# Moving the exponential, the query and key splits and the conversion copies within a step of a fused attention and expert kernel

## The chip, the cores and the metric

One core of one Trainium2 chip. The metric is device time in microseconds (us) of one launch; lower is better. Engines: PE (TensorE), DVE (VectorE), ACT (ScalarE), POOL (GpSimd), and SP, whose queue issues every DMA.

## The reference, cut to what matters

```python
# q, k, v: (8, 12, 448, 64); w_pre, w_post: (12, 12)
scores = scale * np.matmul(q, k.transpose(0, 1, 3, 2))
scores = np.einsum('bhij,hg->bgij', scores, w_pre)        # heads mixed before softmax
scores = scores - np.max(scores, axis=-1, keepdims=True)
attn = np.exp(scores)
attn = attn / (np.sum(attn, axis=-1, keepdims=True) + 1e-09)
attn = np.einsum('bhij,hg->bgij', attn, w_post)           # and after it
attn_out = np.matmul(attn, v)
x = attn_out.transpose(0, 2, 1, 3).reshape(3584, 768)
h = (x @ w1) * (x @ w2) @ w3                              # 768 -> 1024 -> 1024
out = h @ w_out                                           # 1024 -> 768
```

The weights of the second half arrive as 64-bit words that the kernel converts to fp32.

## The kernel before

The work is cut into 360 steps: 8 batches of 45 blocks, each block 10 query rows of all 12 heads, so that a tile is 120 partitions (row and head) by 448 keys. `run` is one loop over the steps with an order of instructions written out by hand: each engine executes its own instructions in the order in which the loop issues them, and waits on semaphores for the others. In step n:

- **mix** (L231, issued at the end of step n-1): PE multiplies the 120x448 raw scores by the block matrix of `w_pre` into a PSUM bank (banks 2 and 3 in turn). From step 20 (`WHOLE`) on, the raw scores are split into a high part `rh` (DVE, L227) and a low part `rl` (POOL, L228), two steps ahead (`split_r`), and three matmuls are made (L239 to L241).
- **softmax** (L243): DVE takes the minimum `mn` of each row (L247; the sign is folded in), then ACT takes the exponential `e` with the row sums `sm` (L250).
- **scale** of block n-1 (L253): DVE adds 1e-9 (`sa`, L259) and takes the reciprocal (`ri`, L260); the 120x120 matrix of `w_post` is multiplied by it into `w2`, on DVE (L263) for n below `LATE` = 107, on ACT (L265) from there on.
- **qk** (L188): PE makes the raw scores of a later batch, 112 queries of one head at a time, in banks 0 and 1 in turn; ACT copies them out (`st`, L199) and SP stores them. The operands of a head come from `split_kq` (L175): three ACT casts (L181 to L183) and two POOL subtractions (`ql` L184, `kk` L185). It is due two or three steps ahead of the head's first use, later where its buffers are still in use.
- **post** of block n-2 (L268): four matmuls with `w2` into bank 4 (`pso`, L273); ACT copies the bank out to `mt` (L279) at the end of the step, in `do_ends`. The next step's `pso` needs bank 4 free, and its own `w2`.
- **av** in a few steps (L294): matmuls with the values (`psa`, L304; 48 in the trace for each such step).
- **advance**: background matmuls, first the folding of two weights into one (`psf`, L362, to step 49), then the experts (`eg`, `eo`, `e...`, to the end). After step 359 these run alone.
- **converting** (L124): weights become fp32 in pieces of up to 384 columns, 40 pieces for the folding and 32 for the experts, in steps 0 to 100, none in steps with av. A piece costs ACT a copy (`two_parts`, L121) and a square (`cm`, L102), POOL a subtraction (L122), and DVE four instructions (`ca`, `cx`, L112 to L116, with the PSUM bank 5 as its scratch). The generator has two halves per step: the first is called before `softmax`, the second after the `qk` copies.

Of the kernel before, what the change touches and what calls it, by code (L numbers as in the profile page):

```python
# [15 lines left out]
B, H, S, D = 8, 12, 448, 64  # L16
# [9 lines left out]
WHOLE = 20  # L26
# [19 lines left out]
class Kernel:  # L46
# [77 lines left out]
    def converting(self, jobs):  # L124

        words, made = [], None
        jobs = list(jobs)
        for n in range(-2, len(jobs) + 1):  # L130
            if n + 2 < len(jobs):
                src = jobs[n + 2][0]
                words.append(self.words(src, f"{self.n_words}"))
                self.n_words += 1
            if made:
                jobs[n - 1][1](made)
                made = None
            if 0 <= n < len(jobs):
                s = words.pop(0)
                m = self.square(s, f"{self.n_made}")  # L140
            yield
            if 0 <= n < len(jobs):
                made = self.to_f32(s, m, f"{self.n_made}")
                self.n_made += 1
            yield
# [94 lines left out]
        nc.tensor.matmul(p[:K, :S], self.wpl[:K, :K], rh[:K], start=False, stop=False)  # L240
        nc.tensor.matmul(p[:K, :S], self.wph[:K, :K], rl[:K], start=False, stop=True)  # L241

    def softmax(self, n):  # L243

        nc, K, p = self.nc, H * self.width(n), self.psm.pop(n)
        mn = self.ep.tile([GI, 1], F32, tag="mn", name=f"mn{n}")
        nc.vector.tensor_reduce(mn[:K], p[:K, :S], axis=AX.X, op=ALU.min)  # L247
        e = self.ep.tile([GI, S], F32, tag="e", name=f"e{n}", bufs=3)
        sm = self.ep.tile([GI, 1], F32, tag="sm", name=f"sm{n}")
        nc.scalar.activation(e[:K], p[:K, :S], AF.Exp, bias=mn[:K], scale=-1.0, accum_out=sm[:K])  # L250
        self.es[n] = (e, sm)
# [490 lines left out]

    def run(self):
        nc, tc = self.nc, self.tc
        self.kqs, self.parts, self.rs, self.rhl, self.psm, self.es, self.w2s = ({} for _ in range(7))
        self.mt, self.vs, self.xs, self.fw = {}, {}, {}, {}
        self.later, self.ends, self.soon = [], [], []
        self.slot, self.free, self.keep, self.x_made, self.n_groups = {}, list(range(N_UP)), [], [0] * B, 0
# [63 lines left out]
        loads, splits, qks, avs, lasts = {}, {}, {}, {}, [-1, -1]  # L812
        for b in range(1, B):
            first, per, ahead = (12, 26 / 48, 2) if b == 1 else ((b - 1) * NB - 6, 45 / 48, 3)
            for u in range(H * NJ):
                h, c = divmod(u, NJ)
                n = first + int(u * per)
# [13 lines left out]
        N = B * NB  # L831
# [29 lines left out]
        def advance(count):  # L861
            nonlocal done
            for _ in range(min(count, total - done)):
                next(background)
                done += 1

        def there(p):

            f, r = divmod(p - 3 - 2 * KF, 3)
            return 2 * KF * 3 * (1 + f) + (0, 9, 18)[r] if f >= 0 else min(max(3 * (p - 3), 0), KF * 3)  # L870
# [3 lines left out]
        def others(p):  # L874
            nc.sync.dma_start(self.kq0s[p][:, JT + S:], self.kq0[p][:, JT + S:])
# [22 lines left out]
        for n in range(N + 6):  # L898
            self.step = n
            if n == GB + 1:  # L900
                self.close("qp")
                self.xp = [self.pool("xp0", 1)]
            if n == SWITCH:
                assert done == total
                next(background, None)
                self.do_ends()
                self.do_soon()
                self.do_later()
                assert not fold_pieces
                self.close("fp")  # L910
                self.wp = self.pool("wp", 5, side="right")
                self.up = self.pool("up", 1, side="right")
                self.xp.append(self.pool("xp1", 1, side="right"))
                background, total, done = self.experts(phases), (E_1 + E_2) * ONE + P_1 * (B - ONE) // 2, 0
            if n == LATE:
                assert done >= E_1
                self.close("xp0", "cx")
                self.xq, self.cb = self.pool("xq", 2), self.pool("cb", 1)
            if n == PAIR:

                assert done >= 2 * E_1 + E_2 and unit_pieces is None and not self.jobs and not self.ys
                self.do_ends()
                self.do_soon()
                self.do_later()
                self.pairs, self.w_ahead = True, 4
                self.close("xp1", "cb", "xq", "cs")
                self.xq = self.pool("xq", 2)
                self.up2 = self.pool("up2", 1, side="right")
                self.free += range(N_UP, NS)
                setup = self.pair_setup(phases)  # L930
            if PAIR <= n < PAIR + 7:
                next(setup, None)
            if LF <= n + LF < N:
                self.fetch(n + LF)
            self.do_later()
            if n + 3 < HP:
                others(n + 3)
            elif 2 * HP - 3 <= n < 2 * HP:
                self.load_v()
            for x in loads.get(n, []):  # L940
                self.load_kq(*x)
            for x in splits.get(n, []):
                self.split_kq(*x, nc.gpsimd, nc.gpsimd)

            p, pieces = self.n_made - 1 if fold_pieces else 2 * KF + 3 * KF, None
            if avs.get(n):
                pass
            elif fold_pieces:
                f = (self.n_made - 1 - 2 * KF) // 3
                if f < 2 or done >= 2 * KF * 3 * (f - 1):  # L950
                    pieces = fold_pieces
                    if next(pieces, self) is self:
                        fold_pieces = pieces = None
            if n < N:
                self.softmax(n)
            if 0 <= n - 1 < N:
                self.scale(n - 1)
            if n + 2 < N:
                self.split_r(n + 2)
            self.do_soon()  # L960
            for x in firsts.get(n, [])[:1]:
                self.later.append(self.qk_first(*x, (next(turn), next(turn))))
            for x in qks.get(n, []):
                store = self.qk(*x, nq % 2, nc.scalar.copy)
                nq += 1
                if store:
                    self.later.append(store)
            if pieces:
                next(pieces)
            elif unit_pieces and not fold_pieces and not avs.get(n):  # L970
                ahead = 1 if n < SWITCH else 2 * done // (3 * K1) + 4 + (done > 0)
                if n_pieces < ahead:
                    n_pieces += 1
                    if next(unit_pieces, self) is self:
                        unit_pieces = None
                    else:
                        next(unit_pieces)
            now = share.get(n, 0)
            if n < SWITCH:

                wanted += now
                now = max(min(there(p), KF * 3 + wanted) - done, 0)
            self.do_sums()

            advance(now // 2)
            if 0 <= n - 2 < N:
                self.post(n - 2)
            for x in firsts.get(n, [])[1:]:
                self.later.append(self.qk_first(*x, (next(turn), next(turn))))
            for x in avs.get(n, []):  # L990
                self.av(*x)
            advance(now - now // 2)
            if n + 1 < N:
                self.mix(n + 1)
            self.do_ends()

        self.do_soon()
        self.do_later()
# [61 lines left out]
```

## Time and profile before

| | |
|---|---|
| time, median of 3 runs | 1638.86 us (1637.82 to 1643.52) |
| the profiled execution | 1637.16 us, of which 1635.4 us are its span from first to last instruction |
| mean granted TensorE clock | 0.991 |
| busy: PE, DVE, ACT, POOL | 97%, 63%, 64%, 65% of the span |
| DMA, mean | 267 GB/s |

The exponentials of step 20, 50 and 110 start at 113.5, 248.7 and 470.3 us, that of step 359 at 1444.8 us; the rest is experts alone. In the trace's rows, `out<-in` names the tiles without their numbers; a timeline's row has the start, the duration, the engine and line, and in brackets how long the engine had been idle and what ended it. A row of the waits has the engine, line and tile that waited, what released it, and then the total in us, the number of waits and the longest. The end of a matmul in the trace is modelled, so that neighbours overlap.

### The profile page before, as it was taken

To read this page: it belongs to the slowest core of one execution; us is meant where nothing else is said; L and a number is where in the kernel's file an instruction comes from. 1 tells how busy PE (TensorE), PEld (TensorE's weight loads), DVE (VectorE), ACT (ScalarE), POOL (GpSimd) and SP (SyncE) were. 2 spreads that over 40 slices of the span, in tenths; PEclk is the share of its full clock that TensorE was granted. 3 is DMA by queue.
4 is the path that set the end of the run, shared out by engine and by line. 5 is a ranking of instruction groups with operands and counts; after the bars stand their busy time and mean duration, and the time that the engine had idled before them with its cause. 6 is when DMAs were issued, how large, how long until landed. Compare 5 with 4: busy or idle time off the path is not lost. (4 is left out here: it accounts for less than half of the span.)

```text
span 1635.4 us, 31769 instructions
## 1 busy us (share of the span) xinstructions
PE 1582.5 (97%) x10528; PEld 1413.9 (86%) x10528; DVE 1030.1 (63%) x2302; ACT 1044.7 (64%) x2497; POOL 1070.2 (65%) x904
## 2 busy tenths in 40 slices
PE   6989998999999999999999999999999999999999
PEld 2479997887898888889999898898999898999988
DVE  5868768778747767863466465755565567634573
ACT  4878767777767777776766666776775554542321
POOL 1347546667657788885576777876675666655774
PEclk7999999999999999999999999999999999999999
DMA  8988869898899999999978887889888866678875
GB/s 270 327 275 271 253 206 298 276 290 271 248 284 305 309 329 309 311 335 303 300 238 284 267 241 240 245 250 314 285 248 246 241 185 205 204 223 301 279 236 175
DMA packets 233906, 436.47 MB, mean 267 GB/s; under 512 B 21838, under 2 KB 159054, under 8 KB 233678
## 3 DMA queue, kind: packets, MB, share of 16 engines
q1 hardware_dynamic: 233742, 434.44, 84.6%
q8 instruction: 83, 1.36, 0.4%
q14 instruction: 81, 0.66, 0.1%
HBM read 300.27 MB, written 134.09 MB: 266 GB/s over the span
## 5 line engine op out<-in xcount | busy, mean ns | idle before, releaser
L228 POOL TENSOR_TENSOR rl<-r,rh 120x448 fp32r<-120x448 f32 (+1 forms) x340 | 425.8, 1253 | 324.8 <-DVE rh L227 97.6
L247 DVE TENSOR_REDUCE mn<-psm 120x1 f32<-120x448 f32 x360 | 224.1, 623 | 410.9 <-PE psm L241 394.8
L250 ACT ACTIVATE e<-psm,mn 120x448 f32<-120x448 f32 x360 | 228.5, 635 | 323.9 <-DVE sa L259 266.7
L273 PEld LDWEIGHTS pso<-w,e 120*112 120x112 f32 (+1 forms) x2880 | 344.7, 177 | 48.5 <-ACT mt L279 34.3
L273 PE MATMUL pso<-w,e 120*112 120x120 f32 (+1 forms) x2880 | 358.3, 267 | 19.3 <-ACT mt L279 19.1
L704 PE MATMUL e<-eh,wu 128*128 128x448 f32 x1008 | 304.8, 372 | 1.1 <-DVE c L658 1.1
L279 ACT COPY mt<-pso 112x480 f32<-112x480 f32 x360 | 207.1, 575 | 13.8 <-PE pso L273 9.8
L704 PEld LDWEIGHTS e<-eh,wu 128*128 128x128 f32 x1008 | 187.2, 188 | 16.3 <-DVE c L658 1.8
L227 DVE CAST rh<-r 120x448 fp32r<-120x448 f32 (+1 forms) x340 | 189.2, 556 | 2.3 <-DMA r<-raw_d 1.5
L704 PE MATMUL e<-el,wu 128*128 128x448 f32 x504 | 187.3, 372 | 2.5 <-POOL el L643 2.5
L199 ACT COPY st<-psq 112x448 f32<-112x448 f32 x336 | 173.0, 527 | 9.6 <-DMA raw_d<-st 6.6
L304 PE MATMUL psa<-mt,v 112*64 112x150 f32 (+1 forms) x2304 | 156.8, 292 | 0.8 <-DMA v<-v 0.8
L184 POOL TENSOR_TENSOR ql<-kq,qh 64x448 fp32r<-64x448 f32 x84 | 98.4, 1172 | 86.6 <-ACT qh L181 69.0
L304 PEld LDWEIGHTS psa<-mt,v 112*64 112x64 f32 x2304 | 143.6, 137 | 6.9 <-DMA v<-v 1.0
L658 DVE TENSOR_TENSOR c<-c,e 128x448 f32<-128x448 f32 x168 | 101.2, 615 | 70.0 <-PE e L704 65.5
L194 PE MATMUL psq<-kk,qh 128*112 128x448 f32 x336 | 125.9, 375 | 7.0 <-ACT st L199 6.9
L239 PE MATMUL psm<-rh,wph 120*120 120x448 f32 (+1 forms) x340 | 129.7, 381 | 0.0
L524 PE MATMUL eg<-xh,wu 128*128 128x448 f32 x384 | 127.4, 381 | 0.0
L241 PE MATMUL psm<-rl,wph 120*120 120x448 f32 (+1 forms) x340 | 123.9, 364 | 0.5 <-POOL rl L228 0.5
L240 PE MATMUL psm<-rh,wpl 120*120 120x448 f32 (+1 forms) x340 | 124.2, 365 | 0.0
L195 PE MATMUL psq<-kk,ql 128*112 128x448 f32 x336 | 122.9, 366 | 0.0
L643 POOL TENSOR_TENSOR el<-x,eh 128x448 fp32r<-128x448 f32 x90 | 106.3, 1201 | 8.5 <-DMA x<-x_d 5.3
(116 smaller groups left out, 3011.8 us busy)
## 6 DMA issues: line engine op xcount, KB each, us to landing
r<-raw_d SPq DMA_DIRECT2D x352, 210.0 KB, 5.3
raw_d<-st SPq DMA_DIRECT2D x168, 392.0 KB, 4.3
wu<-w_d SPq DMA_DIRECT2D x104, 384.0 KB, 5.5
wu<-s_d SPq DMA_DIRECT2D x96, 384.0 KB, 4.7
v<-v SPq DMA_DIRECT2D x144, 224.0 KB, 4.6
wu<-w_d SPq DMA_DIRECT2D x51, 512.0 KB, 6.2
kq<-kq SPq DMA_DIRECT2D x42, 448.0 KB, 6.3
wu<-s_d SPq DMA_DIRECT2D x36, 512.0 KB, 4.4
```

The costliest lines, as they stand in the source:

```text
L194: nc.tensor.matmul(p, qh[:, cols], kk, start=True, stop=False)
L199: copy(st[:, c % 2], p)
L227: nc.vector.tensor_copy(rh[:K], r[:K])
L228: nc.gpsimd.tensor_tensor(rl[:K], r[:K], rh[:K].bitcast(F32), op=ALU.subtract)
L239: nc.tensor.matmul(p[:K, :S], self.wph[:K, :K], rh[:K], start=True, stop=False)
L247: nc.vector.tensor_reduce(mn[:K], p[:K, :S], axis=AX.X, op=ALU.min)
L250: nc.scalar.activation(e[:K], p[:K, :S], AF.Exp, bias=mn[:K], scale=-1.0, accum_out=sm[:K])
L273: nc.tensor.matmul(p[:, j, :, :w], e[:K, j * JT:(j + 1) * JT], w2[:K, :, :w], start=True, stop=True)
L279: self.ends.append((4, lambda: copy(dst, p[:, :, :, :w])))
L304: nc.tensor.matmul(self.psa[rows, g % 3, :W], v[:, j, rows], mt[:, j, 2 * g + s, :W], start=(j == 0), stop=(j == NJ - 1))
L524: nc.tensor.matmul(p, u[:, k % (K1 // 2), x], xs[y][:, k], start=(k == 0 and t == 0), stop=(k == K1 - 1 and t == 2))
L704: nc.tensor.matmul(p, w[:, k, x], ops[m, k][y], start=(k == 0 and t == 0), stop=(k == nk - 1 and t == 2))
```

## The change

`softmax` is cut in two: `largest` (the minimum, DVE) and `exp` (the exponential, ACT). For steps from 20 on, `exp(n)` is issued at the very end of step n, behind the next `mix` and behind `do_ends`; for steps below 20 it stays at the start. `split_kq` moves from the start of a step to its very end, behind `exp`. `split_r` (`rh` on DVE, `rl` on POOL) moves ahead of `scale`. In `converting`, the copy and subtraction of the last piece and the square of this one move from the first half to the second, behind the `qk` copies; what is left in the first half is the load. `scale` still stands ahead of the conversion.

```diff
             if n + 2 < len(jobs):
                 src = jobs[n + 2][0]
                 words.append(self.words(src, f"{self.n_words}"))
                 self.n_words += 1
+            yield
             if made:
                 jobs[n - 1][1](made)
                 made = None
             if 0 <= n < len(jobs):
                 s = words.pop(0)
                 m = self.square(s, f"{self.n_made}")
-            yield
-            if 0 <= n < len(jobs):
                 made = self.to_f32(s, m, f"{self.n_made}")
                 self.n_made += 1
             yield
...
-    def softmax(self, n):
-
-        nc, K, p = self.nc, H * self.width(n), self.psm.pop(n)
+    def largest(self, n):
+
+        nc, K, p = self.nc, H * self.width(n), self.psm[n]
         mn = self.ep.tile([GI, 1], F32, tag="mn", name=f"mn{n}")
         nc.vector.tensor_reduce(mn[:K], p[:K, :S], axis=AX.X, op=ALU.min)
+        self.mns[n] = mn
+
+    def exp(self, n):
+        nc, K, p, mn = self.nc, H * self.width(n), self.psm.pop(n), self.mns.pop(n)
...
-            for x in splits.get(n, []):
-                self.split_kq(*x, nc.gpsimd, nc.gpsimd)
...
             if n < N:
-                self.softmax(n)
+                self.largest(n)
+            if n < WHOLE:
+                self.exp(n)
+            if n + 2 < N:
+                self.split_r(n + 2)
             if 0 <= n - 1 < N:
                 self.scale(n - 1)
-            if n + 2 < N:
-                self.split_r(n + 2)
...
                 self.mix(n + 1)
             self.do_ends()
 
+            if WHOLE <= n < N:
+                self.exp(n)
+            for x in splits.get(n, []):
+                self.split_kq(*x, nc.gpsimd, nc.gpsimd)
+
```

The orders of PE and of SP's queue are the same before and after; DVE, ACT and POOL have the same instructions in another order. Two places show it.

First, DVE in step 52 and the start of step 53 (`mn` is the minimum, `sa`, `ri` and `w` the scaling of the block before, `rh` the high part for two steps on, `ca` and `cx` the conversion). Before:

```order
L247 TENSOR_REDUCE mn_3284<-psm_3275 120x1
L259 TENSOR_SCALAR sa_3289<-sm_3240 120x1
L260 RECIPROCAL ri_3290<-sa_3289 120x1
L263 TENSOR_SCALAR w_3291<-wpo,ri_3290 120x120
L227 CAST rh_3295<-r_3164 120x448
L112 TENSOR_SCALAR ca_3311<-cs_3084 128x384
L113 SCALAR_TENSOR_TENSOR ca_3311<-cs_3084,ca_3311 128x384
L114 SCALAR_TENSOR_TENSOR ca_3311<-cs_3084,ca_3311 128x384
L116 SCALAR_TENSOR_TENSOR cx_3315<-cm_3309,ca_3311 128x384
L247 TENSOR_REDUCE mn_3330<-psm_3322 120x1
```

and after the change:

```order
L246 TENSOR_REDUCE mn_3284<-psm_3265 120x1
L226 CAST rh_3286<-r_3164 120x448
L262 TENSOR_SCALAR sa_3290<-sm_3271 120x1
L263 RECIPROCAL ri_3291<-sa_3290 120x1
L266 TENSOR_SCALAR w_3292<-wpo,ri_3291 120x120
L112 TENSOR_SCALAR ca_3308<-cs_3081 128x384
L113 SCALAR_TENSOR_TENSOR ca_3308<-cs_3081,ca_3308 128x384
L114 SCALAR_TENSOR_TENSOR ca_3308<-cs_3081,ca_3308 128x384
L116 SCALAR_TENSOR_TENSOR cx_3312<-cm_3306,ca_3308 128x384
L246 TENSOR_REDUCE mn_3330<-psm_3319 120x1
```

`rh` has moved from behind `w` to ahead of `sa`; nothing else has moved on DVE.

Second, ACT around step 34, which makes the operands of head 11 of batch 1 (`qh1_11`, `kk1_11`); that head's first scores, `psq1_11_0`, are made in step 35, behind `psq1_10_3`. Before:

```order
L279 COPY mt0_2_2095<-pso31_2169 112x48x10
L181 CAST qh1_11_2189<-kq1_5_1737 64x448
L182 CAST kk1_11_2190<-kq1_5_1737 64x448
L183 CAST qh1_11_2189<-kq1_5_1737 64x448
L121 CAST fw5_2198<-cx31_2035 128x3x128
L102 ACTIVATE cm32_2201<-cs32_1932 128x384
L250 ACTIVATE e34_2205,sm34_2206<-psm34_2180,mn34_2203 120x448
L199 COPY st1_10_0_2159<-psq1_10_1_2219 112x448
L199 COPY st1_10_2_2226<-psq1_10_2_2223 112x448
L279 COPY mt0_2_2095<-pso32_2240 112x48x10
L250 ACTIVATE e35_2263,sm35_2264<-psm35_2252,mn35_2261 120x448
```

and after the change:

```order
L282 COPY mt0_2_2092<-pso31_2166 112x48x10
L253 ACTIVATE e33_2183,sm33_2184<-psm33_2118,mn33_2136 120x448
L198 COPY st1_10_0_2156<-psq1_10_1_2204 112x448
L198 COPY st1_10_2_2211<-psq1_10_2_2208 112x448
L121 CAST fw5_2213<-cx31_2025 128x3x128
L102 ACTIVATE cm32_2216<-cs32_1932 128x384
L282 COPY mt0_2_2092<-pso32_2230 112x48x10
L253 ACTIVATE e34_2247,sm34_2248<-psm34_2177,mn34_2191 120x448
L180 CAST qh1_11_2250<-kq1_5_1737 64x448
L181 CAST kk1_11_2251<-kq1_5_1737 64x448
L182 CAST qh1_11_2250<-kq1_5_1737 64x448
L198 COPY st1_10_2_2211<-psq1_10_3_2273 112x448
```

The casts of the split have moved from the front of the step to behind the step's `mt` copy and its exponential; the conversion's copy and square have moved behind the two score copies.

More of the change, by code (lines that the diff above doesn't have):

```diff
@@ L744, in run @@
         nc, tc = self.nc, self.tc
-        self.kqs, self.parts, self.rs, self.rhl, self.psm, self.es, self.w2s = ({} for _ in range(7))
+        self.kqs, self.parts, self.rs, self.rhl, self.psm, self.mns, self.es, self.w2s = ({} for _ in range(8))
         self.mt, self.vs, self.xs, self.fw = {}, {}, {}, {}
```

## The prediction

> **What bounds the kernel now.** I read the page's busy times first, then the windows by stage, then who waits for whom, then the timeline of one place that waits. The page:
>
> ```profile
> PE 1582.5 (97%) x10528; PEld 1413.9 (86%) x10528; DVE 1030.1 (63%) x2302; ACT 1044.7 (64%) x2497; POOL 1070.2 (65%) x904
> ```
>
> PE works 1582.5 of 1635.4 us, so no order of the others can win more than 53 us, and its gaps lie where the windows show them (steps 20 to 49, 50 to 106, 107 to 201; PE, weight loads, DVE, ACT, POOL busy, clock, DMA share, GB/s):
>
> ```profile
> 112.00:248.00 136.00, 135.24 (x952) 128.28 (x950) 97.56 (x247) 95.88 (x225) 77.21 (x71) 1.00 0.82 249
> 248.00:459.00 211.00, 196.56 (x1386) 173.14 (x1387) 164.80 (x429) 156.48 (x367) 143.27 (x129) 1.00 0.89 280
> 459.00:820.00 361.00, 354.45 (x2534) 322.62 (x2531) 230.97 (x475) 263.43 (x647) 262.48 (x206) 1.00 0.94 309
> ```
>
> The stretch that can be won is steps 50 to 106: PE is idle 211 - 196.6 = 14.4 us there, against 0.8 and 6.6 in its neighbours. What PE waits for there, and behind it from step 107 on:
>
> ```profile
> PE pso L273 <- ACT mt L279: 12.3, 16, 1.6
> PE pso L273 <- ACT mt L279: 5.1, 9, 1.0
> ```
>
> The first `pso` of a step waits for the copy that empties its bank. The timeline of steps 52 and 53 tells why that copy is late:
>
> ```profile
> 256.71 0.57 ACT L279 COPY mt<-pso 112x480 f32<-112x480 f32 x1
> 257.34 1.07 PE L273 MATMUL pso<-w,e 120*112 120x120 f32 x8 [1.58 <-ACT mt L279]
> 258.94 0.64 ACT L250 ACTIVATE e<-psm,mn 120x448 f32<-120x448 f32 x1 [1.66 <-DVE sa L259]
> 260.84 0.56 ACT L279 COPY mt<-pso 112x480 f32<-112x480 f32 x1
> 261.45 1.07 PE L273 MATMUL pso<-w,e 120*112 120x120 f32 x8 [1.41 <-ACT mt L279]
> ```
>
> ACT stands idle for 1.66 us in front of the exponential, because the minimum is late, and the copies behind it, `mt` last, are late with it. The minimum is late because DVE is full:
>
> ```profile
> 258.23 0.62 DVE L247 TENSOR_REDUCE mn<-psm 120x1 f32<-120x448 f32 x1
> 258.76 0.14 DVE L259 TENSOR_SCALAR sa<-sm 120x1 f32<-120x1 f32 x1
> 258.94 0.16 DVE L260 RECIPROCAL ri<-sa 120x1 f32<-120x1 f32 x1
> 259.14 0.28 DVE L263 TENSOR_SCALAR w<-wpo,ri 120x120 f32<-120x120 f32 x1
> 259.34 0.39 DVE L227 CAST rh<-r 120x448 fp32r<-120x448 f32 x1
> 259.64 0.55 DVE L112 TENSOR_SCALAR ca<-cs 128x384 int32<-128x384 int32 x1
> 261.99 0.62 DVE L247 TENSOR_REDUCE mn<-psm 120x1 f32<-120x448 f32 x1
> 259.86 1.14 POOL L228 TENSOR_TENSOR rl<-r,rh 120x448 fp32r<-120x448 f32 x1 [1.33 <-PE psq L195]
> ```
>
> From minimum to minimum DVE needs 3.76 us without a gap when the step has a conversion. So DVE paces these steps, and ACT hands its delay on to PE.
>
> **The change part by part.**
>
> *Exponential last, steps 50 to 106.* It takes the wait for the minimum out of ACT's way to `mt`: `mt` then follows `pso` directly. If that were all, most of the 14.4 us would go. What is late next is `w`, which `pso` of the next step needs, and `rh` is now ahead of it. That has a price on DVE. POOL starts `rl` 0.13 us after `rh` ends (259.34 + 0.39 to 259.86), and this row pair shows what a running POOL subtraction does to `w`:
>
> ```profile
> 124.12 1.16 POOL L228 TENSOR_TENSOR rl<-r,rh 120x448 fp32r<-120x448 f32 x1
> 124.58 0.78 DVE L263 TENSOR_SCALAR w<-wpo,ri 120x120 f32<-120x120 f32 x1
> ```
>
> `w` takes 0.28 us in the rows above; here it ends at 125.36, 0.08 us behind POOL's end at 125.28. Now the new order at step 52: `mn` 258.23, `rh` 258.76 to 259.15, `rl` 259.28 to 260.42, `sa` 259.06, `ri` 259.24, `w` from 259.44. It finds `rl` running and ends at 260.50; the conversion starts at about 260.42 where it started at 259.64. A step with a conversion then costs DVE 3.76 + 0.78 = 4.54 us. The Trainium skill, "SBUF — State Buffer", section "Who interferes with whom", has this as a rule that speaks against the change: a one-source DVE instruction in its two-port mode and a GpSimd instruction lock each other out for the whole instruction, and the order of issue decides who blocks. The same page measured a release 115 ns after the other's end, where this trace has 0.08 us; by it the sum would be 0.035 us x 87 steps = 3 us higher, an estimate.
>
> Summed over the stretch, with the groups by line in this window:
>
> ```profile
> L247 DVE TENSOR_REDUCE mn<-psm 120x1 f32<-120x448 f32 (+1 forms) x58 | 36.0, 621 | 33.9 <-PE psm L241 33.8
> L263 DVE TENSOR_SCALAR w<-wpo,ri 120x120 f32<-120x120 f32 (+1 forms) x58 | 23.0, 396 | 2.0
> L112 DVE TENSOR_SCALAR ca<-cs 128x384 int32<-128x384 int32 x31 | 17.2, 554 | 0.2
> ```
>
> DVE is busy 164.8 us and waits 33.8 us for PE's mix; the other 12 us are short pauses between its instructions. `w` grows from 0.396 to 1.06 us: 58 x 0.66 = 38 us. So DVE needs 164.8 + 12 + 38 = 215 us for a stretch that lasted 211, and it will still stand idle for some 3 us in the long steps with values, where PE is behind: 218 us, **+7**. Bounds: where POOL is busy elsewhere, `rl` comes later and `w` passes; if that holds in 3 of 10 steps, 38 becomes 27 and the term is -4; if DVE never becomes the bound, -13 (14.4 less a little); if each of the 31 conversion steps costs its whole 0.78 us and half of ACT's old waits (7 us of 14.4) remains, less 14.4, 24 + 7 - 14.4 = +17.
>
> In steps 20 to 49 the same 0.6 us a step is hidden: 97.6 + 30 x 0.6 = 116 of 136 us. Zero, at worst +3.
>
> *Splits last.* Where a head has two or more steps until its use this costs nothing: PE's steps of 3 to 5 us cover it. Two heads of batch 1 are split just one step ahead (5 in step 21, 11 in step 34). The latter, now:
>
> ```profile
> 177.26 0.57 ACT L181 CAST qh<-kq 64x448 fp32r<-64x448 f32 x1
> 177.73 0.56 ACT L182 CAST kk<-kq 64x448 fp32r<-64x448 f32 x1
> 177.96 1.15 POOL L184 TENSOR_TENSOR ql<-kq,qh 64x448 fp32r<-64x448 f32 x1 [1.20 <-issue]
> 179.18 1.15 POOL L185 TENSOR_TENSOR kk<-kq,kk 64x448 fp32r<-64x448 f32 x1
> 179.77 0.62 ACT L250 ACTIVATE e<-psm,mn 120x448 f32<-120x448 f32 x1
> 181.22 0.59 ACT L279 COPY mt<-pso 112x480 f32<-112x480 f32 x1
> 183.10 0.36 PE L194 MATMUL psq<-kk,qh 128*112 128x448 f32 x1
> ```
>
> PE needs the operands at 183.10; the last is the second subtraction, ready at 180.33 today. In the new order the chain starts behind `mt`: exponential 181.8, first cast 182.4 to 183.0, `ql` 183.1 (0.13 us later, as above), `kk` 1.22 us behind it, to 185.5. PE waits 185.5 - 183.1 = 2.4 us. Two places, the first a little less because ACT's score copies held PE up there already: **+4.5** (+2 if ACT runs ahead, +6 if POOL is behind).
>
> *Conversion copies later, steps 0 to 19.* Here the exponential stays in front, and there is no `rl`:
>
> ```profile
> 58.60 0.51 ACT L121 CAST fo<-cx 128x384 fp32r<-128x384 f32 x1 [1.16 <-DVE cx L116]
> 59.40 0.89 DVE L263 TENSOR_SCALAR w<-wpo,ri 120x120 f32<-120x120 f32 x1
> ```
>
> The copy no longer blocks ACT ahead of the exponential, and its subtraction no longer meets `w` (0.89 instead of 0.28 us). Against that, ACT's wait for the minimum has nothing left to fill it. **-1** (-4 to +3).
>
> *From step 107 on*, `w` is on ACT, in front of the score copies, and it needs `ri`, which stands behind `rh`:
>
> ```profile
> L227 DVE CAST rh<-r 120x448 fp32r<-120x448 f32 (+1 forms) x251 | 149.3, 595 | 2.1 <-DMA r<-raw_d 1.5 <-issue 0.3 <-POOL s L486 0.3
> ```
>
> So in 253 of 360 steps ACT's first instruction waits for the same minimum as before, plus `rh`, some 0.6 us, instead of the exponential's 0.63. No decoupling, an even exchange: **+1.5** (-4 to +5).
>
> Sum on the profiled execution, 1637.2 us (span 1635.4 plus 1.8 around it; 1.7 below the median of the runs): 1637.2 + 7 + 4.5 - 1 + 1.5 = **1649 us**, 0.6% over the median.
>
> **The rivals.**
>
> *ACT is freed and DVE keeps up (faster).* `w` gets through before `rl`, or the later `w` is still early enough for `pso`. For it: `w` has a whole PE step until it is used. Against it: the row pair above, and a DVE at 78% in this stretch. Of 14.4 us 11 go, early steps give 3, later ones 3, the two split places cost 2: 1637 - 15 = 1622 us. It decides if the mean of `w` in steps 50 to 106 stays under some 0.6 us.
>
> *Gain and price cancel (no change).* POOL is late in part of the steps, and DVE needs 204 us: terms -3, +4.5, -1, +1: 1639 us.
>
> *The later steps pay (slower).* `rh`, held up by POOL, stands before `w` on ACT, and `st`, `mt` and the experts' operands come later in 253 steps. If the waits for `mt` behind step 107 double (+6) on top of half of my sum: 1650 to 1657 us.
>
> **How the numbers follow.** 0.5% of 1638.9 is 8 us, about what a measurement of this kernel can tell from no change: under 1630.7 is faster, over 1647.1 slower. My forecast (1643 to 1660) has 0.42, a quarter of it below 1647; cancelling 0.28, nearly all of it no change; the freed ACT 0.17; the later steps 0.13. That gives faster 0.18, same 0.37, slower 0.45. The range takes in the low edge of the cancelling case and the top of mine: 1629 to 1661, which leaves out most of the freed case and the worst bounds.
>
> **What would show it.** Right: L263's successor near 1 us in steps 50 to 106; DVE over 195 of 211 us there; PE's waits at `pso` named after DVE's `w` instead of ACT's `mt`; two waits of 2 to 3 us at `psq` in steps 22 and 35. Wrong: `w` still under 0.6 us, or a stretch 50 to 106 shorter than 203 us, or PE waits in the later steps that grow by more than 6 us.

## The result and the profile after

| | before | after |
|---|---|---|
| time, median (lowest to highest) | 1638.86 us (1637.82 to 1643.52) | 1678.53 us (1677.72 to 1684.02) |
| span of the profiled execution | 1635.4 us | 1676.7 us |
| mean granted TensorE clock | 0.991 | 0.992 |

The change makes the kernel slower by 2.4%: ratio 1.0244, 95% interval 1.0222 to 1.0266. That is 40 us where the prediction had 10.

The busy times of the changed kernel, from the page:

```profile
PE 1586.1 (95%) x10528; PEld 1415.1 (84%) x10528; DVE 1117.2 (67%) x2302; ACT 1047.8 (62%) x2497; POOL 1062.9 (63%) x904
```

PE does the same work as before (1586 against 1582 us). DVE executes the same 2302 instructions and is busy 87 us longer, so some of them have become longer. The windows by stage (steps 20 to 49, 50 to 106, then 107 on to 855 us; the columns are those of the prediction's windows):

```profile
112.00:254.00 142.00, 136.07 (x948) 128.87 (x947) 112.59 (x243) 97.46 (x224) 76.12 (x71) 0.99 0.78 238
254.00:489.00 235.00, 200.81 (x1387) 176.05 (x1388) 205.65 (x434) 157.62 (x367) 140.05 (x128) 0.99 0.80 250
489.00:855.00 366.00, 355.39 (x2531) 321.57 (x2532) 246.17 (x475) 263.40 (x645) 258.03 (x205) 1.00 0.93 305
```

The middle stretch has grown most. PE's own work there takes 4.3 us more (200.81 against 196.56); the rest of the 24 us is waiting. To set kernels side by side exactly, I cut each trace at the start of the last `mix` matmul of steps 20, 50, 107, 190 and 359. The table below holds the length of each stage before, and for all other kernels the difference from it, in us, each from one profiled execution. That execution took 4 us more than the kernel's median in x2_rh_ahead_alone and x12_rh_behind_in_conversion_steps, 2 more in x5_conv_behind_mt and x8_exp_last_alone, and 3 less in x1_rh_behind:

| kernel | 0-19 | 20-49 | 50-106 | 107-189 | 190-358 | rest |
|---|---|---|---|---|---|---|
| before | 112.4 | 135.0 | 209.8 | 314.5 | 671.6 | 192.0 |
| after | -0.2 | +6.8 | +23.5 | +4.5 | +7.0 | -0.3 |
| x1_rh_behind | +1.0 | +4.3 | +0.1 | -0.4 | +0.8 | -0.3 |
| x2_rh_ahead_alone | +2.4 | +0.3 | +28.5 | +3.1 | +6.4 | 0.0 |
| x3_splits_front | +2.3 | +3.1 | +25.4 | +4.0 | +6.0 | -0.3 |
| x4_w_on_act | +0.6 | +7.1 | +8.9 | +5.0 | +7.0 | -0.3 |
| x5_conv_behind_mt | +1.1 | +7.1 | -1.5 | +0.3 | +0.8 | -0.8 |
| x6_conv_behind_mt_early_splits | +1.9 | -0.3 | -3.6 | -0.1 | -1.6 | -0.7 |
| x8_exp_last_alone | +3.1 | -1.0 | -2.4 | +0.2 | -1.5 | -0.5 |
| x7_post_one_step_later | +0.5 | +16.5 | +21.5 | +2.4 | +2.6 | +2.2 |
| x9_rl_behind_w | +0.9 | +7.9 | +6.7 | +3.8 | +6.9 | -0.6 |
| x11_rh_behind_from_107 | +0.9 | +9.3 | +25.2 | +2.1 | -0.8 | -0.5 |
| x10_later_post_and_conv_behind_mt | +2.4 | +16.6 | +22.4 | +2.6 | +2.7 | +2.2 |
| x12_rh_behind_in_conversion_steps | -0.3 | +7.5 | +2.5 | +7.1 | +8.4 | -0.3 |

The first column moves by up to 3 us between kernels whose instructions there hardly differ, so a difference of 2 or 3 us in one cell says little.

What PE waits for in steps 50 to 106 of the changed kernel:

```profile
PE pso L276 <- DVE w L266: 24.7, 22, 2.6
PE psa L307 <- DVE cx L116: 4.8, 4, 1.2
...
PE pso L276 <- ACT mt L282: 0.3, 1, 0.3
```

The wait for the copy `mt` is gone, 12.3 us before and 0.3 now. The wait for `w` has taken its place with twice the time. The groups by line of DVE in the same window:

```profile
L266 DVE TENSOR_SCALAR w<-wpo,ri 120x120 f32<-120x120 f32 (+1 forms) x59 | 61.6, 1044 | 2.1
L246 DVE TENSOR_REDUCE mn<-psm 120x1 f32<-120x448 f32 (+1 forms) x59 | 36.5, 618 | 19.0 <-PE psm L240 19.0
```

`w` takes 1.04 us instead of 0.396, and DVE still waits 19.0 us for PE's mix. The timeline of DVE in two steps with a conversion shows both the longer `w` and the step that comes of it:

```profile
266.14 0.62 DVE L246 TENSOR_REDUCE mn<-psm 120x1 f32<-120x448 f32 x1
266.67 0.38 DVE L226 CAST rh<-r 120x448 fp32r<-120x448 f32 x1
266.97 0.15 DVE L262 TENSOR_SCALAR sa<-sm 120x1 f32<-120x1 f32 x1
267.15 0.16 DVE L263 RECIPROCAL ri<-sa 120x1 f32<-120x1 f32 x1
267.35 1.14 DVE L266 TENSOR_SCALAR w<-wpo,ri 120x120 f32<-120x120 f32 x1
268.41 0.55 DVE L112 TENSOR_SCALAR ca<-cs 128x384 int32<-128x384 int32 x1
...
270.76 0.62 DVE L246 TENSOR_REDUCE mn<-psm 120x1 f32<-120x448 f32 x1
...
275.30 0.62 DVE L246 TENSOR_REDUCE mn<-psm 120x1 f32<-120x448 f32 x1
```

and POOL and PE beside it:

```profile
267.28 1.13 POOL L227 TENSOR_TENSOR rl<-r,rh 120x448 fp32r<-120x448 f32 x1 [0.58 <-DVE sa L262]
```

```profile
268.64 1.04 PE L276 MATMUL pso<-w,e 120*112 120x120 f32 x8 [2.58 <-DVE w L266]
```

`w` starts 0.07 us after `rl` and ends at 268.49, 0.08 us after it. From minimum to minimum the two steps take 4.62 and 4.54 us, without a gap on DVE. PE stands still for 2.58 us in front of `pso`. Soon after it, from 269.9 to 273.3 us, the granted clock is 0.50, and a mix matmul takes 0.57 us where it took 0.36 before (264.48 us):

```profile
270.72 0.57 PE L239 MATMUL psm<-rh,wpl 120*120 120x448 f32 x1
```

Such stretches are part of the 4.3 us that PE works longer.

In steps 20 to 49 two waits for the late split are what PE shows:

```profile
PE psq L193 <- POOL kk L184: 5.9, 2, 3.8
```

From step 107 to 358 PE's wait for `mt` has nearly doubled. Before, then after:

```profile
PE pso L273 <- ACT mt L279: 6.7, 10, 1.6
```

```profile
PE pso L276 <- ACT mt L282: 12.7, 19, 1.3
```

### The profile page after: what moved, and what is told of

Its sections match the earlier page's. It is cut to its first block, busy times and chain, and to the rows that moved or that the text cites. A ratio compares the mean times of both kernels' runs of the same rounds, so it can differ in the third digit from the quotient of the medians.

```text
span 1676.7 us, 31733 instructions
## 1 busy us (share of the span) xinstructions
PE 1586.1 (95%) x10528; PEld 1415.1 (84%) x10528; DVE 1117.2 (67%) x2302; ACT 1047.8 (62%) x2497; POOL 1062.9 (63%) x904
## 5 line engine op out<-in xcount | busy, mean ns | idle before, releaser
L227 POOL TENSOR_TENSOR rl<-r,rh 120x448 fp32r<-120x448 f32 (+1 forms) x340 | 404.9, 1192 | 330.9 <-PE psq L194 96.4
L268 ACT ACTIVATE w<-wpo,ri 120x120 f32<-120x120 f32 (+1 forms) x253 | 100.0, 395 | 273.3 <-DVE ri L263 272.4
L226 DVE CAST rh<-r 120x448 fp32r<-120x448 f32 (+1 forms) x340 | 196.9, 579 | 1.5 <-DMA r<-raw_d 1.4
L183 POOL TENSOR_TENSOR ql<-kq,qh 64x448 fp32r<-64x448 f32 x84 | 102.8, 1223 | 113.5 <-ACT qh L180 112.4
L307 PEld LDWEIGHTS psa<-mt,v 112*64 112x64 f32 x2304 | 143.6, 137 | 11.1 <-DVE cx L116 5.6
```

The source lines that it names most:

```text
L226: nc.vector.tensor_copy(rh[:K], r[:K])
L227: nc.gpsimd.tensor_tensor(rl[:K], r[:K], rh[:K].bitcast(F32), op=ALU.subtract)
L307: nc.tensor.matmul(self.psa[rows, g % 3, :W], v[:, j, rows], mt[:, j, 2 * g + s, :W], start=(j == 0), stop=(j == NJ - 1))
```

## The experiments

My theory after the result (A in the first runs) was that the order on DVE makes the whole loss: `rl` locks `w` out up to step 106, and `rh` in front of `ri` delays `w` on ACT after it. The first rival (B) was that the late exponential makes `sa` and `w` late. Later runs name their theories anew.

### The parts of the change

**The order on DVE put back** in the changed kernel (x1_rh_behind).

```diff
-            if n + 2 < N:
-                self.split_r(n + 2)
             if 0 <= n - 1 < N:
                 self.scale(n - 1)
+            if n + 2 < N:
+                self.split_r(n + 2)
```

> The changed kernel with one part undone: rh and rl (split_r) issued behind scale again, everything else as changed. Theory A (the order on DVE: rh ahead of sa starts rl, which shuts w out on DVE up to step 106, and a held rh delays w on ACT behind it): the mean of w in steps 50 to 106 falls from 1.04 to under 0.5 us, that stretch from 235 to 200-212 us, the steps from 107 on lose their extra 11 us; 1678 goes to 1625-1645. Theory B (the exponential is late, so sa and w are late whatever rh does): steps 50 to 106 stay over 225 us, the whole over 1665.

Measured: 1645.51 us, ratio 1.0041 (1.0023 to 1.0058), half a us above the expected range. Steps 50 to 106 and all later ones are back at the time before; the 4.3 us left in steps 20 to 49 belong to the late splits. But the exponential is last here, `w` is short, and still nothing is won in steps 50 to 106. Windows, then ACT's waits and DVE's wait for the mix there:

```profile
251.00:463.00 212.00, 199.63 (x1389) 177.07 (x1388) 169.66 (x430) 157.35 (x369) 142.69 (x128) 0.98 0.88 276
```

```profile
ACT wu L121 <- DVE cx L116: 10.1, 9, 2.1
...
ACT e L253 <- DVE mn L246: 2.5, 3, 1.0
```

```profile
L246 DVE TENSOR_REDUCE mn<-psm 120x1 f32<-120x448 f32 (+1 forms) x58 | 35.9, 619 | 30.0 <-PE psm L240 30.0
```

In the kernel before, ACT's waits for the minimum there were these:

```profile
ACT e L250 <- DVE mn L247: 27.2, 24, 2.2
```

They have shrunk from 27.2 to 2.5 us. Now ACT's conversion copy waits, for `cx`, the last of DVE's conversion. Theory A holds against B, but the freed exponential brings no gain in this stretch.

**That order alone**, in the kernel before (x2_rh_ahead_alone).

```diff
+            if n + 2 < N:
+                self.split_r(n + 2)
             if 0 <= n - 1 < N:
                 self.scale(n - 1)
-            if n + 2 < N:
-                self.split_r(n + 2)
```

> The kernel before with one part alone: split_r ahead of scale, nothing else. Theory A: w meets rl here too; w about 1.0 us, steps 50 to 106 grow from 211 by 15 to 25 us; from step 107 on the exponential still stands ahead of w on ACT and covers most of rh, so 0 to 6 us more; 1655-1670 in all. Theory B: within 5 us of before, 1634-1644.

Measured: 1673.44 us, ratio 1.0209 (1.0187 to 1.0232), above what was expected. These two swapped calls bring 28.5 us in steps 50 to 106 and 9.5 us behind them, and 0.3 us in steps 20 to 49. DVE's groups there, and what ends PE's waits:

```profile
L263 DVE TENSOR_SCALAR w<-wpo,ri 120x120 f32<-120x120 f32 (+1 forms) x58 | 58.6, 1011 | 2.0
```

```profile
PE pso L273 <- ACT mt L279: 26.1, 25, 2.4
```

With the exponential still in front, the same loss shows as a wait for `mt`. Which wait is named depends on what stands in front of ACT's copy; how much is lost stays of the same size, 28.5 against 23.5 us.

**The splits put back to the front** of the step, in the changed kernel (x3_splits_front).

```diff
+            for x in splits.get(n, []):
+                self.split_kq(*x, nc.gpsimd, nc.gpsimd)
...
-            for x in splits.get(n, []):
-                self.split_kq(*x, nc.gpsimd, nc.gpsimd)
```

> The changed kernel with the query and key splits at the front of a step again. By the trace the late split of heads 5 and 11 of batch 1 costs 5.9 us of waits at psq (steps 22 and 35), and nothing elsewhere: 1671-1674. If the splits' place mattered for POOL and the expert operands too, steps from 107 on would change by more than 3 us.

Measured: 1677.04 us, ratio 1.0233 (1.0214 to 1.0253). Steps 20 to 49 shorten by 3.7 us (from +6.8 to +3.1) and PE's wait for `kk` is gone there, but the whole is only 1.5 us under the changed kernel: more was expected.

### Where the locked `w` costs

**`w` on ACT** from step 20 on, in the changed kernel (x4_w_on_act).

```diff
-        if n < LATE:
+        if n < WHOLE:
             nc.vector.tensor_scalar_mul(w2[:K, :, :w], wv[:K, :, :w], ri[:K])
```

> The changed kernel with w (the scaling of the w_post matrix) on ACT from step 20 on instead of from 107 on: the lock between w and rl is gone, the order of DVE's rest stays. Theory A: PE's waits for DVE's w in steps 50 to 106 (24.7 us) vanish, what is left there is w on ACT behind a held rh, as in the later steps: 1650-1662. Theory B: w is late for its row sums, wherever it is made: over 1672.

Measured: 1666.48 us, ratio 1.0173 (1.0154 to 1.0191), between the two expectations. 14.6 of the 23.5 us go. What is left is a new wait of ACT, of the kind that the later steps have:

```profile
ACT w L268 <- DVE ri L263: 34.9, 46, 1.5
```

**`rl` kept off `w`** (x9_rl_behind_w): `rh` stays ahead, but its last 8 columns are cast behind `w`, and `rl` needs them.

```diff
-        nc.vector.tensor_copy(rh[:K], r[:K])
-        nc.gpsimd.tensor_tensor(rl[:K], r[:K], rh[:K].bitcast(F32), op=ALU.subtract)
+        cut = S - 8 if n - 2 <= LATE else S
+        nc.vector.tensor_copy(rh[:K, :cut], r[:K, :cut])
...
+    def split_low(self):
...
+        if cut < S:
+            nc.vector.tensor_copy(rh[:K, cut:], r[:K, cut:])
+        nc.gpsimd.tensor_tensor(rl[:K], r[:K], rh[:K].bitcast(F32), op=ALU.subtract)
...
                 self.scale(n - 1)
+            self.split_low()
```

> The changed kernel with rh still ahead of sa on DVE, but its last 8 columns cast behind w, to step 107, so that POOL's rl, which needs all of rh, can't run while w does. Theory A (w is locked out by the running rl, and that is the whole price): the DVE row of w in steps 50 to 106 falls from 1.04 to 0.3-0.5 us, steps 50 to 106 from 233 to 208-217 us, PE's waits for w there from 24.7 to under 5 us, steps 20 to 49 from 141.8 to 138-140; from step 107 on 8 to 13 us over before, as in the changed kernel; the whole at 1651 to 1660. Theory B (rh's own place, some 0.4 us ahead of sa in each step, is the price, locked or not): steps 50 to 106 at 222 us or more, the whole over 1664.

Measured: 1662.07 us, ratio 1.0139 (1.0124 to 1.0154), 2 us above the expected range; steps 50 to 106 take 216.5 us, within it. `w` is short again though `rh` is still ahead of it, and 16.8 of the 23.5 us are gone:

```profile
L276 DVE TENSOR_SCALAR w<-wpo,ri 120x120 f32<-120x120 f32 (+1 forms) x59 | 27.1, 459 | 2.1
...
L237 DVE CAST rh<-r 120x8 fp32r<-120x8 f32 (+1 forms) x59 | 10.4, 176 | 0.0
```

So most of the loss goes with the lock on `w`. How much of the other 6.7 us is the place of `rh` stays open, since the small casts add 10.4 us of work to DVE and the large cast of `rh` is held itself (0.63 us on average). Two expectations failed: PE's waits for `w` were to fall under 5 us, and 11.8 us are left, named after the small cast right behind `w`; steps 20 to 49 were to come down to 138 to 140 us, and they took 142.9.

**`rh` behind `w` in conversion steps only** (x12_rh_behind_in_conversion_steps).

```diff
-            if n + 2 < N:
+            if n + 2 < N and not conv:
                 self.split_r(n + 2)
             if 0 <= n - 1 < N:
                 self.scale(n - 1)
+            if n + 2 < N and conv:
+                self.split_r(n + 2)
```

> The changed kernel with rh behind w again only in the steps that convert a piece (31 of the 57 steps from 50 to 106, 20 of the 30 before them); in the other steps, and in all from 107 on, rh stays ahead of sa and rl locks w out. Theory A3 (only the conversion steps pay: DVE needs their whole length, so each pays the 0.78 us, 31 x 0.78 = 24 us, and the other steps have room on DVE for the locked w): steps 50 to 106 fall from 233 to 208-214 us while w's mean stays over 0.55 us; from step 107 on 8 to 13 us over before, as in the changed kernel; the whole at 1651 to 1659. Rival (each locked w costs its 0.66 us wherever it stands, so the 24 other steps keep their share, some 10 us): steps 50 to 106 at 217 us or more, the whole over 1661.

Measured: 1657.76 us, ratio 1.0112 (1.0096 to 1.0129), and steps 50 to 106 at 212.3 us, as the first theory has it; from step 107 on it lost 15.5 us, more than the 8 to 13 expected. The row of `w`, and the window:

```profile
L266 DVE TENSOR_SCALAR w<-wpo,ri 120x120 f32<-120x120 f32 (+1 forms) x58 | 38.9, 671 | 2.0
```

```profile
257.00:469.00 212.00, 196.54 (x1381) 174.36 (x1379) 180.35 (x425) 155.54 (x363) 140.31 (x127) 0.99 0.87 277
```

`w` is still 0.25 us longer on average than in x1_rh_behind (0.671 against 0.424). DVE works 10.7 us more there (180.35 against 169.66), and the stretch is only 2.4 us longer, because DVE's idle time in front of the mix has shrunk from 30.0 to 21.4 us. As long as the `w` of the conversion steps is short, a locked `w` in the others costs next to nothing. Undoing the 31 takes 21 of the 23.5 us away. No run leaves the 31 locked and undoes the others, so what the 31 cost by themselves is not shown.

**The later steps alone** (x11_rh_behind_from_107): the same swap of the two calls, for n above `LATE`.

```diff
-            if n + 2 < N:
+            if n + 2 < N and n <= LATE:
                 self.split_r(n + 2)
             if 0 <= n - 1 < N:
                 self.scale(n - 1)
+            if n + 2 < N and n > LATE:
+                self.split_r(n + 2)
```

> The changed kernel with the split issued behind scale again from step 108 on; before that as changed. Theory A (the later steps pay for a held rh that stands in front of sa, ri and ACT's w): from step 107 on within -2 and +3 us of before instead of +11.5, steps 50 to 106 unchanged at 231 to 236; the whole at 1664 to 1670. Rival (the later steps carry on what went wrong before them, or pay for the late exponential): still 6 us or more over before from step 107 on, the whole at 1673 or more.

Measured: 1673.27 us, ratio 1.0205 (1.0187 to 1.0222). From step 107 to 358 it takes 1.3 us more than before (2.1 - 0.8) where the changed kernel takes 11.5, as expected. The whole is 3 us above the expected range and just within the rival's, since the steps ahead of 107, which are those of the changed kernel, came out 5 us longer in this profile. PE's wait for `mt` from step 107 on:

```profile
PE pso L276 <- ACT mt L282: 7.3, 9, 1.8
```

### Why a freed ACT wins little

**The conversion behind `mt`** (x5_conv_behind_mt): x1_rh_behind, and for the experts' pieces (from step 50 on) the second half of the conversion, with ACT's copy that took the place of the wait, is issued behind `mt` too.

```diff
-                        next(unit_pieces)
+                        late = 1
...
             self.do_ends()
 
+            if late:
+                next(unit_pieces)
```

> The changed kernel with scale ahead of the split again (as in the run with the old order on DVE, 1645.5 us) and with the conversion's ACT copy, square and DVE instructions issued behind the step's mt copy, ahead of the exponential. Theory A (the wait in front of ACT's mt copy only moved from the exponential to the conversion's copy, which waits for DVE's cx): steps 50 to 106 fall from 209.9 to about 200 us (198 to 205), the whole to 1633 to 1641; the waits of the conversion's copy stay but mt is not behind them. Theory B (DVE as a whole paces steps 50 to 106, wherever ACT waits): steps 50 to 106 stay at 207 to 212 us, the whole at 1642 to 1648.

Measured: 1641.90 us, ratio 1.0017 (1.0007 to 1.0028). The whole lies between the two ranges, but steps 50 to 106 take 208.3 us: theory A falls, theory B has it. PE's waits in the stretch:

```profile
PE psa L307 <- DVE cx L116: 5.4, 4, 1.9
PE pso L276 <- DVE w L266: 4.7, 6, 1.4
...
PE pso L276 <- ACT mt L282: 0.4, 1, 0.4
```

The wait for `mt` is down to 0.4 us, and waits for DVE's own products stand in its place.

**The splits due one step earlier on top** (x6_conv_behind_mt_early_splits).

```diff
-                    splits.setdefault(max(n - ahead, lasts[-2] + 1), []).append((b, h))
+                    splits.setdefault(max(n - ahead - 1, lasts[-2]), []).append((b, h))
```

> The kernel with the conversion behind mt, and the query and key splits due one step earlier. The price of the late splits in steps 20 to 49 (PE's two waits at psq, about 4 us) goes: steps 20 to 49 at 134 to 137 us instead of 139; the rest as in that kernel. Theory A: 1629 to 1637 us in all, faster than the kernel before; theory B: 1638 to 1644.

Measured: 1633.48 us, ratio 0.9968 (0.9955 to 0.9980), 0.3% faster than the kernel before. Steps 20 to 49 fall to 134.7 us: the price of the late splits goes whole. The whole lies in theory A's range, thanks to these steps; steps 50 to 106, of which theory A speaks, still take 206.2 us, and PE is still idle for 206 - 194.1 = 12 us of them, against 14.4 before:

```profile
249.00:455.00 206.00, 194.06 (x1374) 172.30 (x1373) 167.39 (x428) 156.12 (x364) 141.95 (x127) 1.00 0.89 281
```

**The exponential last, alone**, in the kernel before (x8_exp_last_alone): `softmax` cut as in the change, all else as before.

```diff
             if n < N:
-                self.softmax(n)
+                self.largest(n)
+            if n < WHOLE:
+                self.exp(n)
...
+            if WHOLE <= n < N:
+                self.exp(n)
```

> The kernel before with the exponential alone moved to the end of the step from step 20 on; the splits, the conversion copies and the order on DVE as before. Theory A: the exponential's wait for the minimum leaves the front of ACT's queue and the conversion's copy, which waits for cx, takes its place, so steps 50 to 106 stay within 3 us of before (207 to 213) and the whole at 1636 to 1642. Theory B (a late exponential makes sa and w late, and that is a cost of its own): steps 50 to 106 at 214 us or more, the whole over 1643.

Measured: 1633.13 us, ratio 0.9974 (0.9963 to 0.9984). Steps 50 to 106 take 207.4 us, within theory A's range; the whole is 3 us under it. The exponential's move by itself is a gain of 0.3%, some 4 us, and only part of it stands in this stretch.

**`post` one step later** in the changed kernel (x7_post_one_step_later), so that `w` has a step more until PE needs it.

```diff
-        e = self.ep.tile([GI, S], F32, tag="e", name=f"e{n}", bufs=3)
+        e = self.ep.tile([GI, S], F32, tag="e", name=f"e{n}", bufs=4)
...
-            if 0 <= n - 2 < N:
-                self.post(n - 2)
+            if 0 <= n - 3 < N:
+                self.post(n - 3)
```

> The changed kernel with everything behind the exponential's row sums one step further away: post of block n-3 instead of n-2 in step n, four exponential buffers, the values' matmuls and the end one step later. The order on DVE is that of the changed kernel, with rh ahead of sa and w locked out by rl. Theory A (DVE's lag in conversion steps can't be carried into the long steps because PE needs each w in the next step): with one step more, steps 50 to 106 fall from 233 to 215-226 us, the DVE row of w stays near 1.05 us, PE's waits for w fall under 5 us; whole 1660 to 1672. Rival (DVE is the bound in the whole stretch and slack does not help, or the minimum's place in PSUM, not w, is what limits): steps 50 to 106 at 230 us or more, whole over 1674, and the waits move to the mix.

Measured: 1683.26 us, ratio 1.0275 (1.0261 to 1.0289). Theory A falls: no wait for `w` is left, and the stretch still takes 231.3 us. What PE waits for in its place:

```profile
PE pso L276 <- ACT mt L282: 18.0, 16, 2.3
PE psa L307 <- DVE cx L116: 8.6, 5, 2.7
```

The rival had the time right; it had the waits move to the mix, and they moved to ACT's copies. **The conversion behind `mt` on top** (x10_later_post_and_conv_behind_mt; the conversion moved as in x5_conv_behind_mt, the order on DVE that of the changed kernel) takes most of the waits for `mt` away, and those for `cx` grow:

> The kernel with post one step later, and the conversion's ACT copy, square and DVE instructions behind the mt copy as well, so that neither w nor cx of the same step stands in front of PE's next pso. Theory A2 (with w off the path the same lag reached PE through ACT's conversion copy in front of mt): steps 50 to 106 fall from 231 to 215-225 us, the whole to 1664-1676. Rival (the lag also reaches PE through the minimum, the exponential and the two mix banks, so that DVE's need in the conversion steps sets the stretch whatever stands behind it): 50 to 106 at 228 us or more, the whole over 1676.

Measured: 1685.77 us, ratio 1.0281 (1.0266 to 1.0297), steps 50 to 106 at 232.2 us: the rival again. PE's waits now:

```profile
PE psa L307 <- DVE cx L116: 15.6, 6, 5.1
PE psm L238 <- ACT e L253: 4.7, 8, 1.1
PE pso L276 <- ACT mt L282: 4.2, 7, 0.7
```

Three arrangements in which PE waits for three different things (`w`, ACT's `mt`, the conversion's copy with the value matmuls) give 233.3, 231.3 and 232.2 us. DVE is as full in all three: 205.65, 202.71 and 202.46 us of work, and 19.0, 17.3 and 19.3 us idle in front of the mix. The last two kernels also lose 16.5 us in steps 20 to 49, which I did not follow up. The granted clock was lower in both, 0.97 and 0.96 in those steps and 0.96 in steps 50 to 106, where PE worked 203.25 and 205.36 us against 200.81 in the changed kernel. So they show that the length stays when the late product is another one, but part of what a later `post` won may be hidden by the clock.

## Why the prediction was wrong

The direction and the price of one step held, two terms of the sum did not. By the stages the errors are 23.5 - 7 = 16.5, 6.8 - 4.5 = 2.3, -0.2 + 1 = 0.8 and 11.5 - 1.5 = 10.0 us: 29.6 us, the distance from 1649 to 1678.5.

**Exponential last, steps 50 to 106: +7 forecast, +23.5 measured.** The price of one step was right: 4.54 us from minimum to minimum, and the trace has 4.62 and 4.54; `w` at 1.06, and it has 1.04. The step that failed is the sum over the stretch: "So DVE needs 164.8 + 12 + 38 = 215 us for a stretch that lasted 211, and it will still stand idle for some 3 us in the long steps with values". Busy and short pauses came out as said (205.65 + 10), but DVE stood idle for 19.0 us in front of the mix, not for 3. These 16 us are the error of the term. The sum took nearly all of the 33.8 us in which DVE had waited for time that the longer `w` could fill. The timelines show in which steps it lay. Steps 50, 62, 65, 77, 80, 92 and 95 hold the values' matmuls, 31 others a conversion, and 19 neither. Before the change 22.8 us of DVE's idle time lay behind the seven steps with values, 11.1 in the 19 steps and none in the 31. After it 16.0 of the 19.0 us lie behind the seven, and 2.9 in the 19, nearly all of them at the end, where no conversion is left. Only some 15 of the 34 us could be filled, and less than a third of those behind the steps with values.

Step 62 of the changed kernel shows why. PE, then DVE:

```profile
306.19 1.05 PE L276 MATMUL pso<-w,e 120*112 120x120 f32 x8 [1.32 <-DVE w L266]
308.45 3.28 PE L307 MATMUL psa<-mt,v 112*64 112x150 f32 x48 [1.21 <-DVE cx L116]
312.17 0.36 PE L240 MATMUL psm<-rl,wph 120*120 120x448 f32 x1
```

```profile
308.31 0.62 DVE L246 TENSOR_REDUCE mn<-psm 120x1 f32<-120x448 f32 x1
312.57 0.62 DVE L246 TENSOR_REDUCE mn<-psm 120x1 f32<-120x448 f32 x1 [1.99 <-PE psm L240]
```

PE waits first, for the `w` and the `cx` that DVE still owes (`psa` goes to bank 5, the scratch of the conversion). Only behind its 48 matmuls comes the mix that the next minimum needs, and by then DVE has nothing left to do and waits in its turn.

Between two such steps DVE does carry a lag along and make it up. Before the change the minimum of step 53 starts 3.33 us behind the start of its last mix matmul (261.99 against 258.66), that of step 57 only 0.40 us, and step 56, without a conversion, takes DVE 1.75 us from minimum to minimum:

```profile
273.55 0.62 DVE L247 TENSOR_REDUCE mn<-psm 120x1 f32<-120x448 f32 x1
275.30 0.62 DVE L247 TENSOR_REDUCE mn<-psm 120x1 f32<-120x448 f32 x1 [0.25 <-PE psm L241]
```

After the change the minimum stays 2.4 to 6.1 us behind from step 53 to step 62, and DVE does not wait for a mix from step 52 to step 62. DVE's work then sets the time from one step with values to the next, and PE waits for what is left of the lag in the step with values. Cut at the mix, the 31 steps with a conversion grow by 10.8 us in all, the seven with values by 9.6 and the 19 by 3.1. x12_rh_behind_in_conversion_steps (31 steps undone, 21 us back) and x7_post_one_step_later and x10_later_post_and_conv_behind_mt (another product is the late one, the time is nearly the same) agree with that. The prediction's upper bound had 31 x 0.78 = 24 us, as the price of the conversion steps alone; that this comes near 23.5 is not shown to be more than chance.

That bound then took ACT's old waits off again (24 + 7 - 14.4). "If that were all, most of the 14.4 us would go" is refuted: with the exponential last and a short `w`, x1_rh_behind has +0.1 and x8_exp_last_alone -2.4 us. PE's waits for `mt` were for the most part the form in which DVE's full step reached PE, not their cause, as the prediction's own sentence "DVE paces these steps, and ACT hands its delay on to PE" should have told it. Freeing the messenger left the 3.76 us as they were.

The zero for the lock in steps 20 to 49 held: +0.3 in x2_rh_ahead_alone. DVE was busy 107.35 of 134 us there, so the longer `w` found room.

**Splits last: +4.5 forecast, +6.8 measured** in steps 20 to 49, of which x3_splits_front gives back 3.7 and x6_conv_behind_mt_early_splits 7.4 against x5_conv_behind_mt. Two waits at `psq` came, in steps 22 and 35 as forecast, of 3.8 and 2.1 us against 2.4 us twice. The mechanism was right and the size near.

**Conversion copies later, steps 0 to 19: -1 forecast, -0.2 measured**, within its bounds and too small to tell. (The part that moves acts only up to step 49: the two halves of an expert's piece, from step 50 on, both stood behind the `qk` copies already.)

**From step 107 on: +1.5 forecast, +11.5 measured.** The step that failed is "an even exchange". The forecast looked at ACT's first instruction of a step, which waits either way, and took the exponential's 0.63 us that leave the front against the 0.6 us of `rh` that come in. But the swap is the whole cost: x11_rh_behind_from_107 undoes it there, with the exponential still last, and 10.2 of the 11.5 us go; x2_rh_ahead_alone has it without the late exponential and loses 9.5. `rh` ahead of `ri` makes `w` on ACT later in all these steps, and the copies behind it. PE's wait for `mt` carries 6.0 us of it (12.7 - 6.7). PE's waits for POOL's `el` grow too, from 2.5 to 5.5 us, but x11_rh_behind_from_107 has 5.1 us of them without the loss; where the other 5 us go stays open. This was the rival of the later steps, with the sign right and about half of the size (+6). Its reason was half right: `rh` is in the way, but it isn't held up more than before by POOL. Its mean there was 595 ns before and is 606 now:

```profile
L226 DVE CAST rh<-r 120x448 fp32r<-120x448 f32 (+1 forms) x251 | 152.0, 606 | 1.5 <-DMA r<-raw_d 1.4
```

**The rivals.** The freed ACT fails on both of its conditions: `w` was 1.04 us where it needed under 0.6, and where the runs made `w` short, no more than 3.6 us were won in steps 50 to 106. The cancelling case fails with it. Of the signs named ahead, four came (`w` near 1 us, DVE at 205.65 us, PE's waits named after `w`, two waits at `psq`, one of them longer than said), and so did one of those that would make it wrong: PE's waits from step 107 on grew by more than 6 us, from 12.6 to 20.7 in all.

**What stays open.** The two changes that beat the kernel before, x6_conv_behind_mt_early_splits and x8_exp_last_alone, win 5 and 4 us, spread over stages in pieces of 1 to 4 us; the runs don't say which wait that was. That the steps with values settle DVE's lag is read from the traces; no run moved the values' matmuls or gave the conversion's scratch another bank to try it.

## What to carry to other kernels

Before an engine's idle time is spent in a sum, look in which steps it lies, and whether the work can be carried there: most of DVE's lay behind seven steps in which PE and DVE waited for each other in turn, and most of that could not be filled. Ahead of moving the instruction that a wait is named after, ask which engine is without a gap from step to step in those steps; if it is another one, the wait only takes a new name. And where two engines share an operation's path, as DVE and POOL here, the order of two short instructions can cost more than the instructions take: here what starts the other engine's work belongs behind the work that it would lock out.

## What the runs showed of the hardware

- A running POOL subtraction stretched the 120x120 `w` on DVE from 0.28 to 1.04 us on average (steps 50 to 106 of the changed kernel), with the end 0.08 us behind POOL's. It did nothing to the minimum or to the small `sa` and `ri`, which keep their 0.61, 0.14 and 0.16 us, while the cast `rh` between them grows from 0.38 to 0.80. DVE and POOL in a later step of the changed kernel:

```profile
553.07 0.61 DVE L246 TENSOR_REDUCE mn<-psm 120x1 f32<-120x448 f32 x1
553.61 0.80 DVE L226 CAST rh<-r 120x448 fp32r<-120x448 f32 x1
554.33 0.14 DVE L262 TENSOR_SCALAR sa<-sm 120x1 f32<-120x1 f32 x1
554.50 0.16 DVE L263 RECIPROCAL ri<-sa 120x1 f32<-120x1 f32 x1
```

```profile
552.67 1.48 POOL L184 TENSOR_TENSOR kk<-kq,kk 64x448 fp32r<-64x448 f32 x1
554.23 2.29 POOL L227 TENSOR_TENSOR rl<-r,rh 120x448 fp32r<-120x448 f32 x2
```

`rh` ends 0.26 us behind the end of `kk`, a longer gap than that of `w`.
- A cast of 8 columns (x9_rl_behind_w) took 0.176 us on average, one of 448 columns 0.38 us when nothing held it: by an estimate from these two, nearly half of the longer one doesn't depend on its columns.
